# The smaller halves of every second whole unit on GpSimd, as an integer sum less the larger halves

## The chip, the cores and the metric

The kernel runs on one core of one Trainium2 chip. The time is in device microseconds (us), the median of several runs. A profile is one execution of the program; its span reaches from the first to the last profiled instruction. Engines are named as in the profile: PE (TensorE's matmuls), PEld (its weight loads), DVE (VectorE), ACT (ScalarE), POOL (GpSimd), SP (SyncE).

## The reference

Attention that keeps the 32 largest scores of each row, for 8 batches x 8 heads x 576 rows x 64, and behind it a block of layer norm and two matrix products with a residual, all in float32:

```python
def _attn_ref(q, k, v):                      # (8, 8, 576, 64) each
    scores = scale * np.matmul(q, k.transpose(0, 1, 3, 2))
    kth = np.partition(scores, -32, axis=-1)[..., -32:-31]
    scores = np.where(scores >= kth, scores, -1000000000.0)
    scores = scores - np.max(scores, axis=-1, keepdims=True)
    attn = np.exp(scores)
    attn = attn / (np.sum(attn, axis=-1, keepdims=True) + 1e-09)
    return np.matmul(attn, v)

def _moe_ref(x, g_ln, w_ch1, w_ch2):         # x: (8, 576, 512); 512 -> 2048 -> 512
    xn = (x - mean(x)) / np.sqrt(var(x) + 1e-06) * g_ln
    return x + np.maximum(xn @ w_ch1, 0.0) @ w_ch2
```

## The kernel before

The attention is cut into 160 **units**, numbered `u.i`. A whole unit is 128 query rows of two heads (two tiles of 128 x 576 scores); a rest unit holds the last 64 rows of both heads in one tile. There are 128 whole units and 32 rest units. One loop, `for n in range(END)`, takes one step a unit, and in it the work of several units is written out by hand, in an order that each engine keeps: step n selects in unit n (`u`), masks unit n-1 (`mk`), turns or moves unit n-2 (`ex`), makes the scores of unit n+2, and halves unit n+1 (`nxt`) at its very end. Between these the matrix products of the second block are strewn by `fill()`, a few at a time, from a list `todo`, spread over the steps by a planned cost. They come in blocks of 256 rows, and what is left of them when the attention has ended runs at the end of the program.

Finding the 32 largest of 576 scores of a row goes like this on VectorE:

- `halve(u)`, at the end of step n-1: the scores `sc` are two halves of 288. `hi` is their elementwise maximum (L456), `lo` their minimum (L457). `hi` lies in one of two homes, by the unit's parity; `lo` has a single buffer.
- `select(u, 0)`, at the start of step n: MAX8 finds the 8 largest of `hi` (L478) for each of the two tiles, and MATCH_REPLACE8 strikes them out of `hi` (L464; each is preceded by a MATCH_VALUE_LOAD on the same line).
- `select(u, 1)`, in the middle of the step: MAX8 finds the 8 largest of `lo` (L470) and puts them beside `hi`; then again 8 largest of `hi`, and out with them.
- `select(u, 2)` and `select(u, 3)`, later in the step: 8 more each, over `hi` with the 8 of `lo` beside it. The last gives the threshold.

In step n+1 the unit is `mk`: `prepare` scales threshold and bias on ScalarE (L490, L491), `mask` makes a steep step of the scores on ScalarE (L527) and subtracts the scores from it on GpSimd (L530), once for each tile; `watch` keeps, on GpSimd (L497), how the last of the 8 of `lo` stands to the threshold. If it ever shows that 8 were not enough, or not a number that fits, a flag is set and the whole program runs a second time with two rounds of `lo` (`low_rounds=2`, `doubt=None`). Later in the step ScalarE takes the exponentials (`weigh`, L538). In step n+2 TensorE turns the result (L601), or VectorE does so in blocks (`move`, L572) and sends it through memory (`turned`, `pt`) to its place for the product with the values (`values`, L664).

GpSimd has other work in the same queue: the weights' last step, integer additions of 128x512 (`join`, L178), until unit 21, which is `CONVERTING`; the forms of the second weight matrix (`form_pair`, L1034 to L1040); sums of the hidden layer for a seven-product scheme (L911, L912, L913, L917); the residuals and partial sums (L789, L961, L965); centring of rows (L743, L746); copies of rest rows (L700).

These are the lines of the step that the change stands among:

```python
        if mk:
            prepare(mk)
            for t in range(len(mk.tiles)):
                mask(mk, t)
        if mk and doubt is not None:
            watch(mk)
        ...
        if u:
            select(u, 0)
        ...
            select(u, 3)
        if nxt:
            halve(nxt)
```

Of the kernel before, what the change touches and what calls it, by code (L numbers as in the profile page):

```python
# [10 lines left out]
ALU = mybir.AluOpType  # L11
FP32 = mybir.dt.float32
U32 = mybir.dt.uint32
# [16 lines left out]
def compute(  # L30
# [12 lines left out]
    nc = tc.nc  # L43
    P = nc.NUM_PARTITIONS
# [12 lines left out]
    def pool(name, bufs, **kw):  # L57
        return ctx.enter_context(tc.tile_pool(name=name, bufs=bufs, **kw))
# [3 lines left out]
    HALF = S // 2  # L62
# [7 lines left out]
    lopool = pool("lo", 1)  # L70
# [23 lines left out]
    def brief(name):  # L94

        return psps.tile([P, 512], FP32, tag="ps", name=name)
# [345 lines left out]
    def halve(u):  # L442

        nt = len(u.tiles)
        u.lo = lopool.tile([P, 2, HALF], FP32, tag="lo", name="lo")  # L450
        u.hi = hi_homes[u.i % 2]
        sides = int(doubt is not None)
        u.low, u.body = (sides * LOWS + HALF, sides * LOWS) if doubt is None or u.i // 2 % 2 else (0, LOWS)
        a, b = u.sc[:, 0:nt, 0:HALF], u.sc[:, 0:nt, HALF:S]
        lo, hi = u.lo[:, 0:nt], u.hi[:, 0:nt, u.body : u.body + HALF]
        nc.vector.tensor_tensor(hi, a, b, ALU.max)  # L456
        nc.vector.tensor_tensor(lo, a, b, ALU.min)  # L457

    def select(u, i):

# [25 lines left out]
    def prepare(u):  # L486

        nt = len(u.tiles)
        u.bias, u.edge = u.top[:, 0:nt, 0], u.thr[:, 0:nt, 6]
        nc.scalar.mul(u.edge, u.thr[:, 0:nt, 7], STEEP)  # L490
        nc.scalar.mul(u.bias, u.bias, -scale)  # L491

    def watch(u):

        nt = len(u.tiles)
        half, c = u.i // 16 % 2, 1 + 2 * (u.i % 16)
        nc.gpsimd.tensor_tensor(  # L497
            watched[:, half, c : c + nt], u.hi[:, 0:nt, u.low + 7], u.thr[:, 0:nt, 7], ALU.subtract
        )
        if u.i % 16 == 15 or u.i == N - 1:  # L500
            u.ends_watch = True
            u.half = half
# [21 lines left out]
    def mask(u, t):  # L524
        if u.e is None:
            u.e = epool.tile([P, 2, S], FP32, tag="e", name="e")
        nc.scalar.activation(  # L527
            u.e[:, t], u.sc[:, t], AF.Relu, bias=u.edge[:, t : t + 1], scale=-STEEP
        )
        nc.gpsimd.tensor_tensor(u.e[:, t], u.e[:, t], u.sc[:, t], ALU.subtract)  # L530
# [21 lines left out]
    def heads_of(g, h, i0, i1):  # L552
        c0 = h * (J + 1)
        return g.pt[:, i0:i1, c0 : c0 + J]

    def ends_of(g, i0, i1):
        return g.pt[:, i0:i1, J]
# [101 lines left out]
    def values(g):  # L659
        vb = g.job.v  # L660
        av = brief("av")
        for c in range(J):
            for h in range(2):
                nc.tensor.matmul(  # L664
                    av[h * D : (h + 1) * D, 0 : g.nq],
                    vb[:, h * (J + 1) + c, :],
                    heads_of(g, h, 0, g.nq // 32)[:, :, c],
                    start=(c == 0),
                    stop=False,
                )  # L670
        for h in range(2):
            nc.tensor.matmul(  # L672
                av[h * D : (h + 1) * D, 0 : g.nq],
                ends[:, h * D : (h + 1) * D],
                ends_of(g, 0, g.nq // 32),
                start=False, stop=True,
            )
        g.av = av
# [345 lines left out]
    def form_pair(i, part):  # L1024

        lo, hi = slice(2 * i, 2 * i + 2), slice(NF // 2 + 2 * i, NF // 2 + 2 * i + 2)
        b11, b12 = w2[:, lo, 0 : 2 * P], w2[:, lo, 2 * P : DM]
        b21, b22 = w2[:, hi, 0 : 2 * P], w2[:, hi, 2 * P : DM]  # L1030
        tt = nc.gpsimd.tensor_tensor
        t1, t2 = wt[:, 0, lo], wt[:, 1, lo]
        if part == 0:
            tt(t1, b12, b11, ALU.subtract)  # L1034
            tt(t2, b22, t1, ALU.subtract)
            return
        x = xpool.tile([P, 2, DM], FP32, tag="x", name="form")
        t4, t3 = (x[:, s].rearrange("p (f n) -> p f n", f=2) for s in range(2))
        tt(t3, t2, b11, ALU.subtract)
        tt(t4, b21, t2, ALU.subtract)  # L1040
        return i, x

    def keep_pair(made):
        i, x = made
        for s in range(2):
            nc.sync.dma_start(scratch[:, s, i], x[:, s])
        if i == 3:
            kept_forms[0] = now[0]
# [54 lines left out]
    CONVERTING = max(n for n in batches if batches[n]) + 2  # L1103
# [26 lines left out]
    for j in jobs:  # L1130
        if j.hp == NHP - 1:
            b = j.b
# [26 lines left out]
    def at(i):  # L1159
        return units[i] if 0 <= i < N else None  # L1160
# [96 lines left out]
    take_scores(units[0])  # L1257
    load(fresh[1], nc.sync, nc.scalar)
    halve(units[0])
    scores(units[1])  # L1260
    take_scores(units[1])
# [3 lines left out]
    for n in range(END):  # L1265
# [8 lines left out]
        u, nxt, mk = at(n), at(n + 1), at(n - 1)  # L1274
# [14 lines left out]
            scores(x)  # L1289
        if g and not quick:  # L1290
            values(g)
        if mk:
            prepare(mk)
            for t in range(len(mk.tiles)):
                mask(mk, t)
        if mk and doubt is not None:
            watch(mk)
        if all(map(done, ready)):
            if made_pair:
                keep_pair(made_pair.pop())  # L1300
            if pairs_left:
                made = form_pair(*pairs_left.pop(0))
                made_pair.extend([made] if made else [])
            if None not in (kept_forms[0], plain_done[0]) and formed[0] is None:
                formed[0] = n
# [93 lines left out]
        if nxt:  # L1399
            halve(nxt)  # L1400
# [30 lines left out]
@with_exitstack  # L1431
def kernel(
    ctx: ExitStack,
    tc: tile.TileContext,
    *operands: bass.AP,
):
    nc = tc.nc
    doubt = ctx.enter_context(tc.tile_pool(name="doubt", bufs=1)).tile(
        [1, 1], I32, tag="doubt", name="doubt"
    )  # L1440
    compute(tc, *operands, low_rounds=1, doubt=doubt[:])
    again = nc.values_load(
        doubt[:], min_val=0, max_val=1,
        skip_runtime_bounds_check_because="a comparison's result",
    )
    with tc.If(again > 0):
        compute(tc, *operands, low_rounds=2, doubt=None)
# [31 lines left out]
```

## Time and profile before

| | |
|---|---|
| median of 3 runs | 1563.04 us (1561.82 to 1563.74) |
| the profiled execution's own time | 1566.49 us |
| its span | 1564.6 us |
| granted TensorE clock, mean | 0.971 |
| VectorE's minimum, L457, 128x576 | 128 of them, 854 ns mean |
| VectorE's maximum, L456, 128x576 | 128 of them, 857 ns mean |
| GpSimd's mask subtraction, L530, 128x576 | 288 of them, 1437 ns mean |

Rows of groups read: line, engine, operation, what it writes and reads, its shape, how many, then busy time in us and the mean of one in ns, then the engine's idle time just before them and what ended it. Rows of a timeline read: start in us, duration in us, engine, line, operation. Rows of the chain read: start, duration, what. Rows by stretch read: the stretch, its length, the busy time of PE, PEld, DVE, ACT and POOL with the number of instructions in brackets, the granted clock, the share of DMA and its GB/s. A MATMUL's end is modelled, so TensorE can look busy while it works below its rate.

### The profile page before, as it was taken

How to read it: one execution, taken by the hardware profiler on the slowest of the kernel's cores; microseconds unless marked ns; L12 is line 12 of the kernel's file. 1: busy time of each engine (PE TensorE's matmuls, PEld its weight loads, DVE VectorE, ACT ScalarE, POOL GpSimd, SP SyncE). 2: the span in 40 equal slices, each digit the busy share in tenths (PEclk: the TensorE clock that was granted, in tenths of full speed). 3: DMA queues.
4: the chain of work that ended last, by engine and by line, in shares of the span. 5: the costliest groups of instructions: out<-in, count | busy, mean ns of one | idle time of the engine just before them, and what ended most of it. 6: DMA issues, size and time to landing. Idle time of an engine off the chain costs nothing.

```text
span 1564.6 us, 27256 instructions
## 1 busy us (share of the span) xinstructions
PE 1467.7 (94%) x8046; PEld 1108.0 (71%) x8046; DVE 1349.1 (86%) x3873; ACT 1075.5 (69%) x3085; POOL 941.2 (60%) x1302
## 2 busy tenths in 40 slices
PE   3678889999999899999999999999999999999997
PEld 2456447576787677778777777777777777788886
DVE  6998899899889998989988999999999999767000
ACT  5988777786777767777777776867677776554421
POOL 4757776756474666656656556565647475737524
PEclk7789989999999999999999999999999999999998
DMA  6634541567648774686744796666667567464511
GB/s 174 165 100 122 143 114 60 151 157 209 177 127 201 192 204 130 180 207 151 222 119 133 183 225 183 159 171 182 187 173 197 173 173 196 118 173 114 151 35 50
DMA packets 374776, 245.62 MB, mean 157 GB/s; under 512 B 255956, under 2 KB 343512, under 8 KB 374616
## 3 DMA queue, kind: packets, MB, share of 16 engines
q1 hardware_dynamic: 371048, 243.17, 57.9%
q8 instruction: 67, 1.10, 0.3%
q10 hardware_dynamic: 3568, 0.59, 0.3%
q14 instruction: 93, 0.76, 0.2%
HBM read 166.14 MB, written 77.53 MB: 156 GB/s over the span
## 4 chain that ended last, share of the span: by engine, by line
PE 52%; DVE 31%; ACT 5%; DMA 5%; POOL 4%; issue 2%; SPq 1%; DVEq 0%; POOLq 0%; ACTq 0%
PE hps L821 21%; PE ops L981 13%; DVE m L478 10%; DVE hi L464 8%; PE scps L433 6%; PE av L664 5%; DVE sc L572 3%; DVE lo L457 2%; DVE hi L456 2%; PE ops L860 2%; DVE hi L470 2%; PE tp L601 2%; POOL e L530 2%; DMA raw<-in_moe_w_ch_dram 1%; PE av L672 1%
## 5 line engine op out<-in xcount | busy, mean ns | idle before, releaser
L530 POOL TENSOR_TENSOR e<-e,sc 128x576 f32<-128x576 f32 x288 | 408.7, 1437 | 492.6 <-ACT e L527 437.7
L821 PE MATMUL hps<-xT,w 128*128 128x256 f32 x2304 | 542.0, 384 | 1.6 <-ACT xT L781 1.6
L821 PEld LDWEIGHTS hps<-xT,w 128*128 128x128 f32 x2304 | 423.4, 191 | 80.8 <-issue 25.9
L478 DVE MAX8 m<-hi 128x8 f32<-128x296 f32 (+1 forms) x1152 | 472.8, 446 | 1.2
L464 DVE MATCH_REPLACE8 hi<-m,hi 128x288 f32<-128x288 f32 (+1 forms) x864 | 378.0, 443 | 0.0
L981 PE MATMUL ops<-w,h 128*128 128x256 f32 x1280 | 306.9, 385 | 1.3 <-ACT o L946 1.3
L981 PEld LDWEIGHTS ops<-w,h 128*128 128x128 f32 x1280 | 235.0, 191 | 44.8 <-issue 13.4
L414 ACT COPY sc<-scps 128x288 f32<-128x288 f32 x576 | 189.1, 402 | 76.8 <-POOL e L530 56.0
L538 ACT ACTIVATE e<-e,m 128x576 f32<-128x576 f32 x288 | 225.4, 785 | 7.8 <-POOL e L530 5.8
L527 ACT ACTIVATE e<-sc,m 128x576 f32<-128x576 f32 x288 | 209.3, 769 | 0.0
L572 DVE STREAM_TRANSPOSE sc<-e 128x1152 f32<-128x1152 f32 x87 | 119.0, 1367 | 52.7 <-ACT e L538 46.2
L844 ACT ACTIVATE h<-hps 128x512 f32<-128x512 f32 x144 | 86.7, 602 | 111.0 <-PE hps L821 110.4
L664 PE MATMUL av<-pt,vb 128*64 128x256 f32 (+2 forms) x1280 | 150.8, 379 | 9.6 <-DMA pt<-turned 6.2
L664 PEld LDWEIGHTS av<-pt,vb 128*64 128x64 f32 x1280 | 82.2, 142 | 69.6 <-issue 20.7
L456 DVE TENSOR_TENSOR hi<-sc 128x576 f32<-128x576 f32 (+1 forms) x160 | 127.0, 794 | 3.0 <-ACT sc L414 3.0
L457 DVE TENSOR_TENSOR lo<-sc 128x576 f32<-128x576 f32 (+1 forms) x160 | 126.9, 793 | 0.0
L433 PE MATMUL scps<-kT,late_qT 64*128 64x288 f32 (+3 forms) x832 | 119.9, 407 | 0.0
L981 PE MATMUL ops<-wt,s 128*128 128x256 f32 x512 | 119.4, 383 | 0.0
L433 PE MATMUL scps<-kT,qT 64*128 64x288 f32 x512 | 95.1, 465 | 24.6 <-ACT pt L613 9.0
L470 DVE MAX8 hi<-lo 128x8 f32<-128x288 f32 x288 | 117.8, 445 | 0.0
L981 PEld LDWEIGHTS ops<-wt,s 128*128 128x128 f32 x512 | 94.7, 190 | 17.3 <-issue 4.1
L433 PEld LDWEIGHTS scps<-kT,late_qT 64*128 64x128 f32 (+1 forms) x832 | 69.0, 166 | 50.0 <-issue 20.2
(108 smaller groups left out, 1747.2 us busy)
## 6 DMA issues: line engine op xcount, KB each, us to landing
turned<-sc SPq DMA_DIRECT2D x87, 576.0 KB, 4.3
pt<-turned SPq DMA_DIRECT2D x348, 144.0 KB, 3.1
w<-forms SPq DMA_DIRECT2D x128, 256.0 KB, 4.8
vb<-in_v_dram SPq DMA_DIRECT2D x80, 288.0 KB, 4.3
raw<-in_moe_w_ch_dram SPq DMA_DIRECT2D x32, 512.0 KB, 4.7
kT<-kept SPq DMA_DIRECT2D x48, 288.0 KB, 3.8
kept<-kT SPq DMA_DIRECT2D x32, 288.0 KB, 3.7
kqin<-in_k_dram SPq DMA_DIRECT2D x116, 72.0 KB, 2.7
```

What stands on the lines that cost most here:

```text
L414: nc.scalar.copy(u.sc[:, t, s * HALF : (s + 1) * HALF], u.made[s][t][:, 0:HALF])
L433: nc.tensor.matmul(ps[i * R : i * R + ql, o : o + width], qT[r, q0 : q0 + ql], kT[r, k0 : k0 + width], start=True, stop=True,)
L456: nc.vector.tensor_tensor(hi, a, b, ALU.max)
L464: nc.vector.match_replace(x, m[:, t, :], x, LOWEST)
L478: nc.vector.max(m[:, t, :], u.hi[:, t, r0 : r0 + width])
L527: nc.scalar.activation(u.e[:, t], u.sc[:, t], AF.Relu, bias=u.edge[:, t : t + 1], scale=-STEEP)
L530: nc.gpsimd.tensor_tensor(u.e[:, t], u.e[:, t], u.sc[:, t], ALU.subtract)
L538: nc.scalar.activation(u.e[:, t], u.e[:, t], AF.Exp, bias=u.bias[:, t : t + 1], scale=-scale, accum_out=g.den[:, col : col + 1],)
L572: nc.vector.transpose(blocks.rearrange("p (j c n) -> p j c n", j=ni, n=32), u.e[:].rearrange("p t n -> p (t n)").rearrange("p (c j k) -> p ...
L664: nc.tensor.matmul(av[h * D : (h + 1) * D, 0 : g.nq], vb[:, h * (J + 1) + c, :], heads_of(g, h, 0, g.nq // 32)[:, :, c], start=(c == 0), s ...
L821: nc.tensor.matmul(ps[0][:, side * N : (side + 1) * N], w1[:, c, f * P : (f + 1) * P], self.xT[:, c, 0:N], start=(c == 0), stop=(c == NC - 1),
L981: nc.tensor.matmul(bank[name][:, 0:Q], a(j), rhs, start=first and j == 0, stop=(j == G - 1), skip_group_check=not first,)
```

## The change

For whole units with an odd number after unit 21, VectorE no longer takes the minimum. GpSimd adds the bits of the two halves as 32-bit integers into `lo` (`both_halves`), at step n-1 behind the masks and the watch, and at the start of step n, ahead of the masks, subtracts the bits of `hi` from them (`less_larger`). What is left is the bits of the smaller of the two. `lo` is taken from its pool by `both_halves` for these units, by `halve` for the others.

```diff
         nt = len(u.tiles)
-        u.lo = lopool.tile([P, 2, HALF], FP32, tag="lo", name="lo")
+        if not by_difference(u):
+            u.lo = lopool.tile([P, 2, HALF], FP32, tag="lo", name="lo")
...
         nc.vector.tensor_tensor(hi, a, b, ALU.max)
-        nc.vector.tensor_tensor(lo, a, b, ALU.min)
+        if not by_difference(u):
+            nc.vector.tensor_tensor(lo, a, b, ALU.min)
+
+    def by_difference(u):
+        return doubt is not None and not u.rest and u.i > CONVERTING and u.i % 2 == 1
+
+    def both_halves(u):
+        u.lo = lopool.tile([P, 2, HALF], FP32, tag="lo", name="lo")
+        a, b = (u.sc[:, :, c : c + HALF].bitcast(U32) for c in (0, HALF))
+        nc.gpsimd.tensor_tensor(u.lo[:].bitcast(U32), a, b, ALU.add)
+
+    def less_larger(u):
+        lo = u.lo[:].bitcast(U32)
+        hi = u.hi[:, :, u.body : u.body + HALF].bitcast(U32)
+        nc.gpsimd.tensor_tensor(lo, lo, hi, ALU.subtract)
...
         if g and not quick:
             values(g)
+        if u and by_difference(u):
+            less_larger(u)
         if mk:
             prepare(mk)
             for t in range(len(mk.tiles)):
                 mask(mk, t)
         if mk and doubt is not None:
             watch(mk)
+        if nxt and by_difference(nxt):
+            both_halves(nxt)
```

## The prediction

> **What bounds the kernel now.** I read the page's busy shares and its chain of work first, then busy time by stretch, then the timeline around one halving, and last the chain in order of time.
>
> ```profile
> PE 1467.7 (94%) x8046; PEld 1108.0 (71%) x8046; DVE 1349.1 (86%) x3873; ACT 1075.5 (69%) x3085; POOL 941.2 (60%) x1302
> PE 52%; DVE 31%; ACT 5%; DMA 5%; POOL 4%; issue 2%; SPq 1%; DVEq 0%; POOLq 0%; ACTq 0%
> ```
>
> TensorE looks full at 94%, but the chain gives VectorE 31% of the span, and its 86% is an average over unlike stages. The stretches (columns: PE, PEld, DVE, ACT, POOL busy, each with its instructions) separate them:
>
> ```profile
> 283.00:421.00 138.00, 134.51 (x721) 92.84 (x721) 137.31 (x401) 100.18 (x290) 78.36 (x101) 0.99 0.68 180
> 453.00:596.00 143.00, 136.77 (x785) 104.85 (x785) 142.12 (x408) 102.89 (x301) 83.26 (x116) 0.99 0.75 199
> 600.00:825.00 225.00, 222.70 (x1426) 174.83 (x1424) 208.37 (x600) 167.11 (x511) 140.51 (x206) 1.00 0.63 163
> 826.00:1341.00 515.00, 506.08 (x2741) 384.30 (x2738) 512.26 (x1463) 369.50 (x1073) 314.28 (x455) 0.99 0.66 177
> 1341.00:1452.00 111.00, 110.95 (x573) 90.70 (x572) 74.30 (x197) 58.09 (x162) 68.00 (x102) 1.00 0.55 155
> ```
>
> From 283 to 421, 453 to 596 and 826 to 1341 us VectorE is busy 137.31 of 138, 142.12 of 143 and 512.26 of 515 us: it never stops, so any time added to it there moves everything behind. TensorE's 98% in the last of these is stretched work: it gets 2741 instructions through in 515 us (5.3 per us), against 1426 in 225 us (6.3 per us) between 600 and 825, where it is the bound and VectorE has 17 us to spare. After 1341 VectorE is busy 74.30 of 111 us, and the end is TensorE's.
>
> **What goes and what comes.** Fifty-three units are meant: whole, odd, after unit 21 (23, 25, ... 159, without the rest units). Each loses one minimum on VectorE and gains two integer operations on GpSimd of the same 128x576. Their place decides. The subtraction reads `hi` as the maximum left it; `select(u, 0)` then takes two MAX8 of `hi` and overwrites it in the first replacement. So that replacement must now wait for GpSimd, and in the changed program's instruction order it does carry that wait. Before, there was no wait between maximum and replacement. Here is that place before the change, in order of time (start us, us, engine, line, operation; in brackets the idle time before it and what ended it):
>
> ```profile
> 1004.76 0.74 DVE L456 TENSOR_TENSOR hi<-sc 128x576 f32<-128x576 f32 x1
> 1005.42 0.75 DVE L457 TENSOR_TENSOR lo<-sc 128x576 f32<-128x576 f32 x1
> 1006.09 0.81 DVE L478 MAX8 m<-hi 128x8 f32<-128x288 f32 x2
> 1006.82 0.07 DVE L464 MATCH_VALUE_LOAD hi<-m,hi 128x8 f32 x1
> 1007.48 2.79 POOL L530 TENSOR_TENSOR e<-e,sc 128x576 f32<-128x576 f32 x2 [4.74 <-ACT e L527]
> 1007.66 0.81 DVE L470 MAX8 hi<-lo 128x8 f32<-128x288 f32 x2
> ```
>
> The minimum's slot is 1006.09 - 1005.42 = 0.67 us: that is all the change can take from an undisturbed unit. Behind it 0.73 us of MAX8 (1006.09 to 1006.82) is all the cover that the subtraction has. What the subtraction costs is bounded by GpSimd's rows:
>
> ```profile
> L530 POOL TENSOR_TENSOR e<-e,sc 128x576 f32<-128x576 f32 x288 | 408.7, 1437 | 492.6 <-ACT e L527 437.7 <-PE scps L433 26.6 <-DVE m L478 17.5
> L178 POOL TENSOR_TENSOR w<-wt 128x512 uint32<-128x512 uint32 x20 | 25.1, 1277 | 0.0
> L746 POOL TENSOR_SCALAR x<-x,less 128x512 f32<-128x512 f32 x30 | 26.0, 868 | 3.1
> 1316.62 0.18 DVE L738 BATCH_NORM_AGGREGATE mv<-st 128x2 f32<-128x6 f32 x1
> 1316.89 0.19 POOL L743 TENSOR_SCALAR less<-mv 128x1 f32<-128x1 f32 x1 [4.17 <-DVE mv L738]
> ```
>
> The nearest row, a subtraction of the same shape, means 1437 ns; two of them take 2.79 us, so 1.41 us when nothing disturbs them. The integer addition runs at the same rate (1277 x 576/512 = 1437). The far lower end is the one-input row, 868 x 576/512 = 977 ns; above I allow 1.9 us. I take 1.41. A handover from VectorE to GpSimd is 1316.89 - 1316.80 = 0.09 us, and I take as much back. Counted from the end of `hi` (1005.50), the subtraction is ready at 0.09 + 1.41 + 0.09 = 1.59 us; without the minimum VectorE reaches the replacement at 0.65 us (5.42 - 5.50 + 0.73). It stalls 0.94 and has saved 0.67: **an undisturbed unit loses 0.27 us**, even with GpSimd idle.
>
> One rule of the Trainium skill leans the other way:
>
> ```profile
> L457 DVE TENSOR_TENSOR lo<-sc 128x576 f32<-128x576 f32 x105 | 91.0, 867 | 0.0
> 1277.67 1.40 POOL L530 TENSOR_TENSOR e<-e,sc 128x576 f32<-128x576 f32 x1
> 1278.42 1.27 DVE L456 TENSOR_TENSOR hi<-sc 128x576 f32<-128x576 f32 x1
> ```
>
> The minimum means 867 ns between 240 and 1440 us against 0.75 undisturbed; beside a GpSimd subtraction a two-input operation took 1.27. The Trainium skill ("SBUF — State Buffer", "Who interferes with whom") says that a VectorE operation with two SBUF inputs and a GpSimd one that reads SBUF shut each other out, while VectorE operations with one input don't; the trace agrees. By that rule each removed minimum is worth about 0.12 us more, an estimate of 4 us over 33 units.
>
> **GpSimd's queue.** That price holds only if GpSimd is free when `hi` is done. Its queue is in order: the subtraction stands behind all that step n-1 left there and ahead of both masks of its own step, and the addition adds 1.41 us behind the watch in step n-1 (its wait for the old `lo` costs little: the masks ahead of it end at 1010.27, `lo` was read from 1007.66). Two units at which GpSimd is far behind, each followed by VectorE's next idle time:
>
> ```profile
> 243.55 0.74 DVE L456 TENSOR_TENSOR hi<-sc 128x576 f32<-128x576 f32 x1
> 250.17 1.27 POOL L1040 TENSOR_TENSOR form<-w,wt 128x512 f32<-128x512 f32 x1
> 279.33 1.38 DVE L572 STREAM_TRANSPOSE sc<-e 128x1152 f32<-128x1152 f32 x1 [4.51 <-ACT e L538]
> 436.28 0.74 DVE L456 TENSOR_TENSOR hi<-sc 128x576 f32<-128x576 f32 x1
> 443.46 0.24 POOL L700 COPY oTr<-oT 128x64 f32<-128x64 f32 x1
> 453.22 1.38 DVE L572 STREAM_TRANSPOSE sc<-e 128x1152 f32<-128x1152 f32 x1 [4.11 <-ACT e L538]
> ```
>
> Unit 23: `hi` ends at 244.29; GpSimd has cleared its queue at 251.44, with the addition at 252.85, 8.56 late. A late unit loses that lateness + 1.41 + 0.09 - 0.65 - 0.67 = lateness + 0.18, here 8.7 us. Unit 45: 437.02 against 443.70 + 1.41, so 8.3 us. VectorE was ahead there and paid for it later by waiting 4.51 and 4.11 us; those waits absorb that much. About 5 us (with a little from unit 25) enter the first unbroken stretch and 4.2 the second.
>
> In the third the late units are 91, 117, 123, 127, 133, 135, 141 and 147, eight in all; first and last:
>
> ```profile
> 828.15 1.96 DVE L456 TENSOR_TENSOR hi<-sc 128x576 f32<-128x576 f32 x1
> 830.13 1.24 POOL L965 TENSOR_TENSOR o<-o,t 128x256 f32<-128x256 f32 x1
> 1285.84 4.40 POOL L917 TENSOR_TENSOR h<-h,s 128x128 f32<-128x128 f32 x8
> 1287.83 0.75 DVE L456 TENSOR_TENSOR hi<-sc 128x576 f32<-128x576 f32 x1
> 1288.50 1.01 DVE L457 TENSOR_TENSOR lo<-sc 128x576 f32<-128x576 f32 x1
> ```
>
> Unit 91: 830.11 against 831.37 + 1.41, late by 2.67, a loss of 2.85. Unit 147: 1288.58 against 1290.24 + 1.41, late by 3.07, and since the minimum that goes held 0.93 us (to the MAX8 at 1289.43) a loss of 3.0. Read likewise, the six between lose 2.0, 3.5, 0.5, 1.8, 2.5 and 1.0: 17.2 in all.
>
> Last, GpSimd itself is on the chain once:
>
> ```profile
> 634.12 2.61 POOL e L530 x2
> 637.05 4.34 POOL h L917 x8
> 641.39 0.18 POOL oTr L700
> 641.57 2.73 POOL e L530 x2
> ```
>
> Unit 67's addition falls in front of L917 and its subtraction in front of the masks at 641.57: 2 x 1.41 = 2.8 us onto the chain.
>
> **The sum.** First stretch: 5 entering, five undisturbed units (29 to 37) at 0.27, 1.1 for unit 39: 7.5. Second: 4.2, five (47 to 55) at 0.27: 5.6 (unit 47's own lateness is covered by the 4.2; after 547 the chain is TensorE's). Third: 17.2 and fourteen undisturbed at 0.27: 21.0. The chain at 634: 2.8. Together 36.9 us. Against the profiled execution's own 1566.49 us (span 1564.6) that makes 1603.4; that execution lies 3.45 us above the median of 1563.04, so the median goes to **1600 us**. Stalls elsewhere, 600 to 825 and after 1341, I cost at nothing: VectorE's idle 17 us and, after 1341, 37 of 111 us cover them; if that cover fails they are rival 2.
>
> **The rivals.** (1) GpSimd's lateness doesn't add up, since a VectorE that comes later finds the queue emptier: only the 0.27 remains, on 33 units of the unbroken stretches, 9 us: 1572. For it, GpSimd is busy 314 of 515 us; against it, lateness comes in bursts such as the eight L917 above. (2) Nothing is absorbed: the losses of all 53 units read as above add up to some 120 us (23's 8.7 and 147's 3.0 among them): 1683. Against it stand the idle times quoted. (3) Faster: if the in-place integer subtraction ran at the one-input rate, 0.98 us, the undisturbed unit would win 0.16 instead of losing 0.27, and if GpSimd is then on time 33 of them give 5 us: 1558. The deciding point is 1.14 us; the row of the same shape and the integer row speak against it. (4) TensorE is the bound after all and hides the stalls: 1563; the 5.3 against 6.3 instructions per us speak against it. (5) The halves come out inexact, the doubt that `watch` collects is set, and the whole computation runs again: over 3100. The integer addition is in the trace (L178), a subtraction isn't. The Trainium skill ("GPSIMD Engine Reference", "Engine selection") calls an all-32-bit integer addition exact and wrapping, the ordinary path fp32, and says nothing of subtraction; no run here shows it.
>
> **How the numbers follow.** Forecast 0.62, rival 1 0.15, rival 2 0.09, rival 3 0.06, rival 4 0.06, rival 5 0.02. The range runs from 1568, just below rival 1, to 1645, about half of what rival 2 adds beyond the forecast; it leaves out rivals 3, 4, 5 and part of 2. Faster by over 0.2% (3.1 us, about what a measurement of this kernel can tell from no change) is rival 3, 0.06; within it rival 4, 0.06; the rest, 0.88, is slower.
>
> **What would show it.** In the changed profile: VectorE idle in front of the replacement's line, released by GpSimd's subtraction, about 50 times, 0.9 us at the least and several us at the late units; VectorE's total busy time down by some 40 to 45 us, GpSimd's up by 150; the subtraction's row near 1.41 us; the attention's last unit some 35 us later. I am wrong if those waits are short, if the subtraction's row is near 1 us, or if the waits are there and the end hasn't moved.

## The result, and the profile after

The changed kernel takes 1604.51 us (median of 4 runs, 1601.58 to 1609.18); the kernel before, 1562.43 us beside it. The ratio is 1.0271, with a 95% interval of 1.0242 to 1.0301: 42 us slower. The profiled execution took 1606.68 us, with a span of 1604.9 us.

The page of the changed kernel, busy shares, the chain by engine, and two groups (its line numbers are higher: the maximum is L457, the replacement L485, the MAX8 L499, the MAX8 of `lo` L491, the mask's subtraction L551, the eight late sums L938; the new addition is L472, the new subtraction L478):

```profile
PE 1483.9 (92%) x8046; PEld 1117.6 (70%) x8046; DVE 1312.1 (82%) x3820; ACT 1076.4 (67%) x3085; POOL 1075.6 (67%) x1408
PE 38%; DVE 33%; POOL 13%; DMA 6%; ACT 5%; issue 3%; SPq 2%; ACTq 0%; DVEq 0%; POOLq 0%
L485 DVE MATCH_VALUE_LOAD hi<-m,hi 128x8 f32 x864 | 76.0, 88 | 120.0 <-POOL lo L478 116.7
L478 POOL TENSOR_TENSOR lo<-lo,hi 128x576 uint32<-128x576 uint32 x53 | 74.6, 1408 | 63.5 <-DVE hi L457 63.4
```

VectorE is busy 37 us less than before and yet not sooner done. It stood idle 116.7 us in front of the replacement, and what released it was the new subtraction. The subtraction itself is as long as any of this shape, 1408 ns. On the chain GpSimd went from 4% to 13% and TensorE from 52% to 38%.

What VectorE waited for, by the view of waits (total us, times, longest), before:

```profile
DVE sc L572 <- ACT e L538: 46.2, 10, 8.5
DVE st L737 <- ACT x L686: 36.2, 6, 20.2
```

and after:

```profile
DVE hi L485 <- POOL lo L478: 116.7, 53, 15.9
DVE st L758 <- ACT x L707: 36.0, 6, 20.2
DVE sc L593 <- ACT e L559: 15.3, 6, 5.1
```

So its account closes: 116.7 us of new waits, less 37.0 us of work, less 39.4 us of other idle time, is the 40.3 us by which the span is longer. Of the 39.4 us, 30.9 are waits for ScalarE's exponentials (46.2 - 15.3). The waits for rows of the second block (`st`) did not shrink.

The place of the prediction's first timeline, now at an undisturbed unit of the change (109), VectorE and GpSimd in order of time:

```profile
1008.98 0.76 DVE L457 TENSOR_TENSOR hi<-sc 128x576 f32<-128x576 f32 x1
1009.78 0.82 DVE L499 MAX8 m<-hi 128x8 f32<-128x288 f32 x2
1009.89 1.42 POOL L478 TENSOR_TENSOR lo<-lo,hi 128x576 uint32<-128x576 uint32 x1 [3.50 <-DVE hi L457]
1011.34 0.09 DVE L485 MATCH_VALUE_LOAD hi<-m,hi 128x8 f32 x1 [0.74 <-POOL lo L478]
```

GpSimd had been idle for 3.50 us and began 0.15 us after `hi` was done; still VectorE waited 0.74 us. From the start of the maximum to the first replacement it is 1011.34 - 1008.98 = 2.36 us, against 1006.82 - 1004.76 = 2.06 us before. So this unit lost 0.3 us although all went well; up to 1341 us the other undisturbed units lost 0.15 to 0.31 us, but for two, 29 with 0.50 and 111 with 0.66. At a late unit, the first one (23):

```profile
246.69 2.78 POOL L551 TENSOR_TENSOR e<-e,sc 128x576 f32<-128x576 f32 x2 [7.86 <-ACT e L548]
249.58 1.40 POOL L472 TENSOR_TENSOR lo<-sc 128x576 uint32<-128x576 uint32 x1
250.95 1.26 POOL L1060 TENSOR_TENSOR form<-wt,w 128x512 f32<-128x512 f32 x1
252.18 1.26 POOL L1061 TENSOR_TENSOR form<-w,wt 128x512 f32<-128x512 f32 x1
253.41 1.39 POOL L478 TENSOR_TENSOR lo<-lo,hi 128x576 uint32<-128x576 uint32 x1
254.84 0.09 DVE L485 MATCH_VALUE_LOAD hi<-m,hi 128x8 f32 x1 [9.06 <-POOL lo L478]
```

The subtraction stands behind two masks, the addition and both forms; VectorE waits 9.06 us for it. GpSimd was not short of time here: it had itself been idle for 7.86 us in front of the masks, until ScalarE's result came, and what stood behind them waited too.

Where the time was lost is read from one instruction, the maximum, at four units (40, 57, 91 and 150; 40 is a rest unit, hence the shape). Before:

```profile
402.83 0.43 DVE L456 TENSOR_TENSOR hi<-sc 128x288 f32<-128x288 f32 x1
550.61 0.74 DVE L456 TENSOR_TENSOR hi<-sc 128x576 f32<-128x576 f32 x1
...
1318.23 0.74 DVE L456 TENSOR_TENSOR hi<-sc 128x576 f32<-128x576 f32 x1
```

and after:

```profile
410.10 0.46 DVE L457 TENSOR_TENSOR hi<-sc 128x288 f32<-128x288 f32 x1
562.73 0.74 DVE L457 TENSOR_TENSOR hi<-sc 128x576 f32<-128x576 f32 x1
850.40 1.98 DVE L457 TENSOR_TENSOR hi<-sc 128x576 f32<-128x576 f32 x1
1355.68 0.74 DVE L457 TENSOR_TENSOR hi<-sc 128x576 f32<-128x576 f32 x1
```

The lag is 7.3 us at unit 40, 12.1 at unit 57, 22.3 at unit 91 (828.15 before) and 37.5 at unit 150; the span ends 40.3 us later.

### The profile page after: what moved, and what is told of

Same layout as the page of the kernel before. It is cut to its first block, busy times and chain, and to the rows that moved or that the text cites. A ratio compares the mean times of both kernels' runs of the same rounds, so it can differ in the third digit from the quotient of the medians.

```text
span 1604.9 us, 27359 instructions
## 1 busy us (share of the span) xinstructions
PE 1483.9 (92%) x8046; PEld 1117.6 (70%) x8046; DVE 1312.1 (82%) x3820; ACT 1076.4 (67%) x3085; POOL 1075.6 (67%) x1408
## 4 chain that ended last, share of the span: by engine, by line
PE 38%; DVE 33%; POOL 13%; DMA 6%; ACT 5%; issue 3%; SPq 2%; ACTq 0%; DVEq 0%; POOLq 0%
PE hps L842 18%; DVE m L499 10%; PE ops L1002 10%; DVE hi L485 10%; PE scps L433 4%; DVE sc L593 4%; PE av L685 3%; DVE hi L491 3%; POOL e L551 3%; POOL lo L478 2%; DVE hi L457 2%; DVE lo L459 2%; ACT e L548 1%; DMA raw<-in_moe_w_ch_dram 1%; PE tp L622 1%
## 5 line engine op out<-in xcount | busy, mean ns | idle before, releaser
L551 POOL TENSOR_TENSOR e<-e,sc 128x576 f32<-128x576 f32 x288 | 405.5, 1427 | 347.4 <-ACT e L548 304.4
L499 DVE MAX8 m<-hi 128x8 f32<-128x296 f32 (+1 forms) x1152 | 479.1, 457 | 3.0
L485 DVE MATCH_REPLACE8 hi<-m,hi 128x288 f32<-128x288 f32 (+1 forms) x864 | 382.5, 454 | 0.0
L1002 PE MATMUL ops<-w,h 128*128 128x256 f32 x1280 | 312.9, 390 | 4.5 <-ACT o L967 2.8
L1002 PEld LDWEIGHTS ops<-w,h 128*128 128x128 f32 x1280 | 238.3, 194 | 49.8 <-issue 13.5
L485 DVE MATCH_VALUE_LOAD hi<-m,hi 128x8 f32 x864 | 76.0, 88 | 120.0 <-POOL lo L478 116.7
L685 PE MATMUL av<-pt,vb 128*64 128x256 f32 (+2 forms) x1280 | 151.4, 380 | 12.8 <-ACT den L571 5.0
L511 ACT ACTIVATE m<-m 128x2 f32<-128x2 f32 (+1 forms) x160 | 33.0, 206 | 153.7 <-DVE m L499 153.5
L593 DVE STREAM_TRANSPOSE sc<-e 128x1152 f32<-128x1152 f32 x87 | 119.8, 1377 | 15.3 <-ACT e L559 15.3
L457 DVE TENSOR_TENSOR hi<-sc 128x576 f32<-128x576 f32 (+1 forms) x160 | 125.0, 781 | 3.0 <-ACT sc L414 3.0
L491 DVE MAX8 hi<-lo 128x8 f32<-128x288 f32 x288 | 119.1, 453 | 0.0
L478 POOL TENSOR_TENSOR lo<-lo,hi 128x576 uint32<-128x576 uint32 x53 | 74.6, 1408 | 63.5 <-DVE hi L457 63.4
```

Of the source, the lines that this page charges most:

```text
L485: nc.vector.match_replace(x, m[:, t, :], x, LOWEST)
L491: nc.vector.max(u.hi[:, t, o : o + 8], u.lo[:, t])
L499: nc.vector.max(m[:, t, :], u.hi[:, t, r0 : r0 + width])
L593: nc.vector.transpose(blocks.rearrange("p (j c n) -> p j c n", j=ni, n=32), u.e[:].rearrange("p t n -> p (t n)").rearrange("p (c j k) -> p ...
L685: nc.tensor.matmul(av[h * D : (h + 1) * D, 0 : g.nq], vb[:, h * (J + 1) + c, :], heads_of(g, h, 0, g.nq // 32)[:, :, c], start=(c == 0), s ...
L1002: nc.tensor.matmul(bank[name][:, 0:Q], a(j), rhs, start=first and j == 0, stop=(j == G - 1), skip_group_check=not first,)
```

## The experiments

Theory W is the prediction's: VectorE loses by waiting for GpSimd's subtraction, 0.27 us at the least and more where GpSimd's queue is late, and those losses reach the end where VectorE never stops. Rival L: the loss is GpSimd's load, that is the 150 us of work added to its queue. Each kernel ran beside the kernel before on the same chip, and ratios are to that.

**The minimum gone, nothing in its place.** For the 53 units `lo` is one half of `sc`, both GpSimd operations are dropped, and `watch` compares two thresholds:

```diff
-        u.lo = lopool.tile([P, 2, HALF], FP32, tag="lo", name="lo")
-        a, b = (u.sc[:, :, c : c + HALF].bitcast(U32) for c in (0, HALF))
-        nc.gpsimd.tensor_tensor(u.lo[:].bitcast(U32), a, b, ALU.add)
+        u.lo = u.sc[:, :, 0:HALF]
...
-        if u and by_difference(u):
-            less_larger(u)
```

> The 53 units have neither the minimum on VectorE nor any operation on GpSimd; MAX8 of lo reads one half of the scores instead, and the watch compares two thresholds of these units. So the smaller halves are left out, and what is timed is the most that the change could have won. Theory W (VectorE is the bound in the three unbroken stretches; the loss came from its waits for GpSimd's subtraction): 33 units in those stretches at 0.67 us, 22 us faster than before, about 1540. Rival T (TensorE is the bound, and VectorE's time does not count): 1562, as before.

1551.11 us, ratio 0.9922 (0.9906 to 0.9939): 12 us faster, not 22. VectorE's time does count, against rival T, but less than the count of slots says:

```profile
PE 66%; DVE 19%; ACT 5%; DMA 4%; POOL 3%; issue 1%; SPq 1%; ACTq 0%; DVEq 0%; POOLq 0%
```

TensorE's share of the chain went from 52% to 66%, and VectorE, which now came earlier, waited longer: 54.3 us for the exponentials instead of 46.2, and 40.7 us for rows instead of 36.2. Taking time from VectorE hands the bound to TensorE. So the most that this change could have won is 12 us.

**Both GpSimd operations, but the second does not read `hi`.**

```diff
-        hi = u.hi[:, :, u.body : u.body + HALF].bitcast(U32)
-        nc.gpsimd.tensor_tensor(lo, lo, hi, ALU.subtract)
+        a = u.sc[:, :, 0:HALF].bitcast(U32)
+        nc.gpsimd.tensor_tensor(lo, a, a, ALU.subtract)
```

> Both GpSimd operations stay at their places and of their size, but the second takes one half of the scores from itself and does not read hi; lo is then zero, so the smaller halves are left out. GpSimd's load is that of the changed kernel; the wait of the first replacement goes, and VectorE needs lo only at the MAX8 of lo. Theory W: an undisturbed unit wins 0.67 us, a late one still loses its lateness less 0.55: about 1568, over 30 us faster than the change. Rival L (the loss is GpSimd's load: 150 us more in its queue delays masks, sums and residuals, and the wait only shows it): still about 1600.

1573.70 us, ratio 1.0064 (1.0047 to 1.0080): 31 us less than the changed kernel; theory W had 1568, rival L 1600. GpSimd is busy for 1071.0 us, 1075.6 in the changed kernel; the second operation turned out shorter, 1170 ns instead of 1408, which is 13 us of GpSimd's time and not enough for 31. VectorE's waits for GpSimd:

```profile
DVE hi L491 <- POOL lo L478: 75.2, 24, 14.7
```

24 waits instead of 53, now at the MAX8 of `lo`: the undisturbed ones are gone, the late ones stay.

**One GpSimd operation.** The addition's place takes a subtraction of one half from itself, `less_larger` is dropped.

```diff
-        nc.gpsimd.tensor_tensor(u.lo[:].bitcast(U32), a, b, ALU.add)
+        nc.gpsimd.tensor_tensor(u.lo[:].bitcast(U32), a, a, ALU.subtract)
...
-        if u and by_difference(u):
-            less_larger(u)
```

> Only the first GpSimd operation, at its place in the step before, and it takes one half of the scores from itself: lo is zero, the smaller halves are left out, the second operation and the wait for it are gone. This is the time that a minimum on GpSimd in one operation would have. Theory W: every undisturbed unit wins 0.67 us, late ones lose little: about 1548. Rival L: half of the load, half of the loss, about 1583.

1556.05 us, ratio 0.9948 (0.9930 to 0.9965). VectorE waits 12.6 us for it, four times. Of the 12 us that are there to be had this keeps 7. Half of rival L's loss would have been 1583 (the one operation took 1155 ns, not 1408, so its load is somewhat under half).

**Parts of the change.** Only `by_difference` is narrowed, by `u.i`: first the nine units from 65 to 89, then the 22 from 91 to 149, and 28 units at which GpSimd was on time.

```diff
-        return doubt is not None and not u.rest and u.i > CONVERTING and u.i % 2 == 1
+        return doubt is not None and not u.rest and u.i > CONVERTING and u.i % 2 == 1 and (65 <= u.i <= 89)
```

> The change for the nine units 65 to 89 alone, between 600 and 825 us, where VectorE had 17 us to spare. Nothing is left out. The prediction costed that stretch at 2.8 us (GpSimd on the chain at unit 67) and let VectorE's spare time cover the rest: 1565. The trace of the changed kernel has unit 57 12.1 us late and unit 89 22.2 us late, which would make it 10 us: 1572.

> The change for the 22 units 91 to 149 alone, the third unbroken stretch; nothing is left out. The prediction's term for it was 21.0 us: 1584. In the changed kernel's trace the halving of unit 91 is 22.3 us late and that of unit 151 is 37.5 us late, so 15 us: 1578. If the loss were GpSimd's load, 22 of 53 units would carry 22/53 of 42 us, 17 us: 1580.

> The change for 28 units at which GpSimd's queue was empty or nearly so when hi was done (29 to 37, 49 to 55, 59, 69, 71, 79, 81, 95, 97, 101 to 111, 115, 121, 129, 139, 145, 149); nothing is left out. Theory W: only the undisturbed price is left, 0.27 us for each of the 23 of them that lie in the unbroken stretches: 6 us, 1569. Rival L: 28 of 53 units carry 28/53 of the loss, 22 us: 1585. Rival P (the minimum's 0.67 us is won, since the wait is hidden elsewhere): 1550.

The nine units: 1572.50 us, ratio 1.0059 (1.0042 to 1.0076), +9 us. The 22 units: 1580.12 us, ratio 1.0100 (1.0086 to 1.0115), +16 us; this can't tell the theories apart, since rival L gave 17. The 28 units: 1573.77 us, ratio 1.0054 (1.0041 to 1.0066), +8 us by the ratio and +10 by the medians, where theory W gave 6 and rival L 22. Two units, 29 and 79, were not on time after all. At unit 29 VectorE waited 2.34 us for the last of these:

```profile
305.99 0.69 POOL L767 TENSOR_SCALAR x<-x,less 128x512 f32<-128x512 f32 x1
306.65 0.19 POOL L764 TENSOR_SCALAR less<-mv 128x1 f32<-128x1 f32 x1
306.94 0.69 POOL L767 TENSOR_SCALAR x<-x,less 128x512 f32<-128x512 f32 x1
307.60 1.41 POOL L478 TENSOR_TENSOR lo<-lo,hi 128x576 uint32<-128x576 uint32 x1
```

In the full change VectorE had been delayed by units 23 and 25 and came to unit 29 when the queue was nearly clear (it waited 1.02 us); alone, it came early. A queue's lateness belongs to the pace of both engines, not to the unit.

**The subtraction in two pieces**, one for each tile, at the same 28 units:

```diff
-        nc.gpsimd.tensor_tensor(lo, lo, hi, ALU.subtract)
+        for t in range(2):
+            nc.gpsimd.tensor_tensor(lo[:, t], lo[:, t], hi[:, t], ALU.subtract)
```

> The same 28 units, with the subtraction in two instructions of 128x288, one for each tile, so that the first replacement waits only for the first; nothing is left out. Theory W: replacement 1 starts at about 0.09 + 0.75 + 0.09 = 0.93 us behind hi instead of 1.59, replacement 2 waits for the second at about 1.65: the unit's loss falls from 0.27 to about 0 us, so 1563, some 6 us faster than with the subtraction in one. Rival L: GpSimd's load is the same or a little more: no faster than the one in one piece.

1567.93 us, ratio 1.0028 (1.0019 to 1.0038): 6 us faster than in one piece by the medians, 4 by the ratios, with GpSimd busy for 7 us more (1021.1 against 1014.1). The first replacement (L486 here) now starts at 1.64 us behind the maximum's start and the second waits a quarter of a microsecond:

```profile
1035.48 0.73 DVE L457 TENSOR_TENSOR hi<-sc 128x576 f32<-128x576 f32 x1
1036.29 1.56 POOL L479 TENSOR_TENSOR lo<-lo,hi 128x288 uint32<-128x288 uint32 x2 [1.85 <-DVE hi L457]
1037.12 0.09 DVE L486 MATCH_VALUE_LOAD hi<-m,hi 128x8 f32 x1
1037.88 0.09 DVE L486 MATCH_VALUE_LOAD hi<-m,hi 128x8 f32 x1 [0.24 <-POOL lo L479]
```

**More cover between maximum and replacement.** Where VectorE transposes a moved unit in the same step, that transpose is placed ahead of the first MAX8: first for 12 units, then for 18 of either parity, then for all 53 of the change (27 of them have such a transpose).

```diff
+        ahead_of_it = moved and u is not None and by_difference(u)
+        if ahead_of_it:
+            move(ex)
         if u:
             select(u, 0)
...
-        if moved:
+        if moved and not ahead_of_it:
             move(ex)
```

> Twelve of the 28 units, those in whose step VectorE also transposes a moved unit; that transpose (1.37 us) is placed ahead of the first MAX8, so that it and the two MAX8 lie between the maximum and the first replacement; nothing is left out. Theory W: the wait disappears (cover 0.73 + 1.3 us against 1.59) and each unit wins 0.67 us, 8 us at the most; with about half of VectorE's savings reaching the end, as in the kernel without the minimum (12 of 22 us), 4 us: 1559. If the transposes then wait for ScalarE's exponentials instead, no gain or a loss: 1563 to 1570.

> The form with the transpose placed between the maximum and the first replacement, now for 18 units of either parity (30, 32, 35, 38, 50, 52, 55, 59, 97, 104, 106, 108, 111, 120, 126, 129, 138, 148), chosen by GpSimd being on time and a moved unit in the same step; nothing is left out. Theory W: 18 times 0.67 us less on VectorE, of which about half reaches the end: 6 us, 1557. If six more units' load on GpSimd makes others late: 1560 to 1565.

> The change for all 53 units, with one thing moved: in the 27 of them in whose step VectorE transposes a moved unit, that transpose lies ahead of the first MAX8. GpSimd's operations are the same in number, size and order; nothing is left out. Theory W: at these 27 units up to 0.94 us of the wait (undisturbed) or 1.3 us (late) is covered, 25 to 35 us less waiting, of which half or more reaches the end: 1575 to 1588. Rival L (GpSimd's load): no difference, 1604. If the transposes come too early for ScalarE's exponentials they wait themselves, and little is won: 1595 to 1604.

With 12 units: 1561.12 us, ratio 0.9982 (0.9970 to 0.9993), 2.5 us faster than the kernel before. The wait has gone (0.6 us in all):

```profile
L485 DVE MATCH_VALUE_LOAD hi<-m,hi 128x8 f32 x864 | 65.9, 76 | 3.9 <-POOL lo L478 0.6
```

```profile
356.58 0.73 DVE L457 TENSOR_TENSOR hi<-sc 128x576 f32<-128x576 f32 x1
357.24 1.36 DVE L593 STREAM_TRANSPOSE sc<-e 128x1152 f32<-128x1152 f32 x1
358.53 0.77 DVE L499 MAX8 m<-hi 128x8 f32<-128x288 f32 x2
359.23 0.07 DVE L485 MATCH_VALUE_LOAD hi<-m,hi 128x8 f32 x1
```

With 18 units: 1563.69 us, ratio 0.9999 (0.9987 to 1.0011), no difference, where 1557 was expected. VectorE waits for the subtraction only once, for 1.09 us, so the saving was lost elsewhere. Part of it shows: four of the transposes that now come early wait themselves for ScalarE's exponentials, where they waited for nothing before, together 3.5 us. The longest two:

```profile
313.50 1.38 DVE L593 STREAM_TRANSPOSE sc<-e 128x1152 f32<-128x1152 f32 x1 [1.39 <-ACT e L559]
331.82 1.38 DVE L593 STREAM_TRANSPOSE sc<-e 128x1152 f32<-128x1152 f32 x1 [1.10 <-ACT e L559]
```

Two waits for rows near 599 and 699 us grew as well, from 3.42 to 4.64 and from 2.40 to 4.14 us. The rest stays open. With all 53: 1583.82 us, ratio 1.0128 (1.0091 to 1.0165), some 21 us less than the changed kernel (22 by the ratios) with the same GpSimd instructions in the same order. By the waits:

```profile
DVE hi L485 <- POOL lo L478: 63.7, 33, 9.1
DVE sc L593 <- ACT e L559: 35.2, 9, 8.3
DVE sc L593 <- POOL s L933: 13.5, 1, 13.5
```

VectorE waits 53 us less for the subtraction than in the changed kernel (63.7 against 116.7). 31 us of the 53 lie behind unit 150, where TensorE has the bound, and there longer waits in front of the transposes took their place (the last two lines). Up to the maximum of unit 151 VectorE waits 22 us less (62.7 against 85.1), and that maximum comes 19.5 us earlier (1345.42 against 1364.96). GpSimd's load is the same, so rival L as the cause of the whole loss is out. What placing the transposes earlier does by itself, with the minimum left on VectorE, was not run; the 18 units, which won nothing, speak against its being the gain.

**Why VectorE's spare time did not cover 600 to 825 us.** The nine units once more, in two parts.

> The change for units 65, 77 and 89 alone, in each of which GpSimd is far behind right after VectorE's waits at 600, 615, 700 and 799 us, so that those waits lie ahead of the stalls and cannot cover them; nothing is left out. Theory C (what counts is whether an idle time of VectorE follows the stall; only the wait at 825 us follows one, unit 89's): nearly all of the nine units' loss, 8 to 9 us: 1571. Rival G (the loss comes from GpSimd's own time on the chain at unit 67): nearly nothing here, 1563.

> The other six of the nine, 67, 69, 71, 79, 81 and 83; nothing is left out. Theory C: little, 0 to 3 us, 1565 (unit 67, late without 65's stall ahead of it, may add some). Rival G: most of the nine units' loss, 1571.

1568.73 us, ratio 1.0034 (1.0023 to 1.0045), and 1568.74 us, ratio 1.0026 (1.0014 to 1.0039): about 5 and 4 us, so neither theory holds alone. In the first, VectorE waits 7.35, 4.85 and 2.82 us for GpSimd, and of these 15.0 us a lag of 4.8 is left at unit 91: other waits of VectorE shrank, the one of 4.82 us at 825 to 1.52 and one of 2.4 at 615 to nothing, while the two for rows did not (2.66 against 2.40 at 700, 4.88 against 4.75 at 799). In the second, unit 67 alone:

```profile
637.42 0.09 DVE L485 MATCH_VALUE_LOAD hi<-m,hi 128x8 f32 x1 [4.54 <-POOL lo L478]
655.45 0.09 DVE L485 MATCH_VALUE_LOAD hi<-m,hi 128x8 f32 x1 [0.74 <-POOL lo L478]
672.15 0.09 DVE L485 MATCH_VALUE_LOAD hi<-m,hi 128x8 f32 x1 [0.73 <-POOL lo L478]
704.88 0.70 DVE L758 BATCH_NORM_STATS2 st<-x 128x6 f32<-128x512 f32 x1 [2.84 <-ACT x L707]
```

But for the change's own waits VectorE's next idle time comes 67 us later, for rows that TensorE and ScalarE make, and it is as long as before (2.84 against 2.40): those rows were late as well. One wait of 0.97 us for a DMA, at 690.56 before, did go. Little more was covered: the lag grew by 4.1 us right behind unit 67 and was no smaller at 72.

## Why the prediction was right, point by point

Forecast 1600, measured 1604.5; the sum of 37 us against 42. By its steps:

- **The wait of the first replacement** was the decisive reading, and it is what the profile shows, 53 times. The undisturbed price came out as worked: 2.36 - 2.06 = 0.3 us against 0.27, with the subtraction at 1.41 us. Only the wait itself is shorter than the 0.9 us that was named as its sign, 0.66 to 0.74 at most of these units: the MAX8 that now reads `hi` right behind the maximum starts 0.80 us after it (1008.98 to 1009.78), where the minimum started 0.66 us after it, and the prediction had let the MAX8 simply move up. The two-piece subtraction and the covered replacement each move it as the cover of 0.73 us says.
- **First and second stretch**: 7.5 and 5.6 us against a lag of 7.3 at unit 40, and of 6.9 at unit 45 (443.18 against 436.28) growing to 12.1 at 57, which is 5.2. Right: unit 23 lost 8.6 us from maximum to replacement (10.67 - 2.06) where 8.7 was worked out, and the two waits of 4.51 and 4.11 us that were to absorb such losses are gone in the changed profile, where a transpose first waits at 847.62.
- **The third stretch** was put too high: 21.0 against 37.5 - 22.3 = 15.2 us (16 with those units alone). The term that was mis-sized is the eight late units. By their time from maximum to first replacement, after less before, they lost 12.8 us, not 17.2 (first and last: unit 91 5.47 - 3.29, unit 147 4.17 - 2.33); the undisturbed ones lost 3.7, as against 3.8. Lateness had been read at VectorE's old pace. That a VectorE which comes later finds the queue shorter, which is rival 1 in part, is the likely reason but not shown: with the 22 units alone, where VectorE came without the 22 us of delay, the eight waits were no longer (unit 91 2.64 in both, unit 147 1.70 against 2.53). Unit 147, worked out at 3.0, lost 1.8: the eight sums in front of it took 3.89 us instead of 4.40.
- **600 to 825 us** is the step that failed: 2.8 us was forecast, and VectorE's 17 idle us were to cover the rest; the lag grew by 22.3 - 12.1 = 10.2 us from unit 57 on (1.6 of it at units 57 and 59, ahead of 600 us), and the nine units alone cost 9. Idle time was cover only where it followed the stall and did not move with it. That TensorE's bound here was not firm enough to hide a late VectorE is argued from this, not shown by a run of its own. The two errors, +5.8 and -7.4, nearly cancelled, so it is by luck that the total is better than its terms.
- **After 1341 us** little was lost, where nothing was costed: 37.5 us of lag at unit 150, 40.3 at the end. The last unit's maximum is 44.5 us late (1480.99 against 1436.47), more than the 35 forecast. VectorE's waits of up to 15.9 us there were mostly hidden by TensorE's remaining products: from unit 150 on TensorE is idle for 12.9 us, 11.2 before.
- **The rivals.** 1 (1572), 2 (1683) and 4 (1563) are out by the time; 3 is out by the subtraction's row of 1408 ns; 5 did not come, the program ran once. That VectorE and GpSimd shut each other out was weighed at 4 us; no run here separates it.
- VectorE's busy time fell by 37 us, not 40 to 45: the forecast counted whole rows of the minimum, 0.75 to 0.87 us, but the end of a row overlaps the next one, and an undisturbed minimum holds VectorE for 0.67 us; 53 of them make 35.5. GpSimd's rose by 134 us, not 150: the 53 additions and 53 subtractions took 149.4 us, and its other rows got shorter.

## What to carry to other kernels

Before work is moved to another engine, ask what the old engine does next with the same data: an operation that reads a tile which is overwritten in place soon after turns into a wait, and what lies between the two is all its cover. Widen that cover (another piece of the engine's own work between, or the moved operation in pieces) and count the other engine's queue ahead of it at the pace that the change will set, not at the old one. In this kernel, spare time of an engine was worth something only behind the stall, and only if what ended it was not late for the same reason. And an engine with idle time can still be late: its queue keeps its order, and one operation that waits holds up all behind it.

## What the runs showed of the hardware that was not expected

An integer subtraction on GpSimd whose two inputs are the same half of a tile took 1155 to 1170 ns, against 1408 ns with two different inputs of the same shape. VectorE starts a MAX8 that reads the maximum's result 0.77 to 0.81 us after the maximum's start, and an operation that does not read it 0.66 us after. And VectorE's rows are about 2% longer in some profiles than in others, throughout the execution, with the same kernel lines: 450 against 440 ns for the same replacement, in the changed kernel's profile and in those of the four experiments that ran on one chip, not in those of the eight on two others. The starts of successive instructions lie 0.36 us apart in both, so this cost no time.
